# Column sums of a 32x32 softmax on VectorE in place of a masked fp32 product on TensorE

## The chip, the core and the metric

The kernel runs on one core of a Trainium2 chip. The core has four engines that matter here, each with its own instruction queue worked in order: TensorE (PE: matmuls, with its weight loads shown apart as PEld), VectorE (DVE), ScalarE (ACT) and GpSimd (POOL, which here only builds masks and issues DMAs). SyncE (SP) issues DMAs alone. TensorE writes to PSUM; the other compute engines bring the results to SBUF. The metric is the device time of one execution in microseconds (us).

## The reference, cut to what matters

Eight batches of eight heads go through a Nystrom attention with 32 landmarks, and its output through an MLP with a squared ReLU.

```python
A  = sm(q, k_lm)       # 576 x 32
Bm = sm(q_lm, k_lm)    # 32 x 32, softmax over its rows
C  = sm(q_lm, k)       # 32 x 576
Z  = Bm.transpose(0, 1, 3, 2) / (np.linalg.norm(Bm, ord=1, axis=(-2, -1), keepdims=True)
                                 * np.linalg.norm(Bm, ord=np.inf, axis=(-2, -1), keepdims=True) + 1e-06)
for _ in range(6):
    Z = 2 * Z - Z @ Bm @ Z
attn = A @ Z @ C @ v
out  = square(maximum(attn_rows @ w_in, 0)) @ w_out
```

The change concerns the starting scale of `Z`. Each row of `Bm` sums to one, so the `inf` norm is one up to rounding, and the kernel uses the 1-norm alone: the largest column sum of each 32x32 matrix.

## The kernel before, in words

**Layout.** The eight heads of a batch lie as two groups of four: partition 32a+i, group qd holds row i of head 4*qd+a. `BB` is an fp32 tile of 128 x 2 x 2 x 32: `BB[:, 1]` holds the landmark softmax (rows on partitions), `BB[:, 0]` its transpose in blocks of 32x32 (line 288). `blk` is the 128 x 128 block-diagonal mask of ones (four blocks of 32), in fp32, and `blk_bf` the same in bf16.

**Stages of a batch.** `attention(b)` is a generator. It makes the segment means (line 244), the landmark scores (line 274, `Exp` on ACT at line 277), the softmax (lines 283 to 288 on DVE), then `inverse_begin` and `inverse_first`, three `joint_step`s, one `last_joint_step` and two `newton_step`s, with the large scores (line 392), sums, transposes and the product with `v` (`c_values`, line 453) as side work between them. Its result is `G` (line 575 and its copies at 581 to 589), with which `mlp_in(b)` makes `h` on PE (line 603), `r` on ACT (line 609) and the square `gT` on DVE (line 610). `mlp_out(b)` multiplies `gT` by `w_out` (line 632, 16 matmuls of 128x512 to one output tile).

**Order.** Batch 0's attention runs alone at the start, in the order in which it is written (three engines are on a manual schedule there), with small filler matmuls (`warm`, line 201) in PE's gaps. From then on `mlp_in(b)` and `mlp_out(b)` on PE are interleaved with `attention(b+1)`, by a loop that advances the generator a step at a time; the framework's scheduler settles the final order of the instructions. Batches 1 and 2 transpose q and k on PE (lines 218 and 228, copied out at 501 to 512); batches 3 to 7 have it done by DMA, issued from SP (lines 189 and 195) after DVE's `nat` copies (line 187), which are pinned behind the first joint step of the batch before.

**Buffers.** All small products and transposes share the PSUM tag `n`, three buffers in rotation. `h` has two, `ops` one, `r` (SBUF) three.

**The lines the change touches.** `inverse_begin` (lines 324 to 338) multiplies the fp32 mask by the fp32 softmax (line 326): `colps[p, qd, m]` is then the sum of column m of p's head, the same in all 32 rows of that head. DVE copies the transposed softmax to bf16 (`btc`, line 330), spreads it to a block-diagonal stationary operand (`BT`, line 307; batch 0 takes `btc` as it is, in 32x32 pieces), takes the maximum over m from PSUM (`n1`, line 333), adds 1e-6 (line 335) and takes the reciprocal (`rc`, line 337). `inverse_first` multiplies `BT` by `btc` on PE (line 316, here called the nu product), scales the result and the softmax by `rc` (lines 343 and 345, `EY`), and spreads the first half to `ED`, the stationary operand of the first joint step.

Of the kernel before, what the change touches and what calls it, by code (L numbers as in the profile page):

```python
# [8 lines left out]
P = 128  # L9
AF = mybir.ActivationFunctionType  # L10
ALU = mybir.AluOpType
AX = mybir.AxisListType

BF16 = mybir.dt.bfloat16
F32 = mybir.dt.float32
# [5 lines left out]
M = 32  # L21
# [13 lines left out]
def kernel(  # L35
# [9 lines left out]
    nc = tc.nc  # L45

    const = ctx.enter_context(tc.tile_pool(name="const", bufs=1))
# [3 lines left out]
    small = ctx.enter_context(tc.tile_pool(name="small", bufs=2))  # L51
# [64 lines left out]
    def band(t, pattern, base, mult):  # L116
        return nc.gpsimd.affine_select(out=t, in_=t, pattern=pattern, compare_op=ALU.is_ge,
                                       fill=0.0, base=base, channel_multiplier=mult)
# [11 lines left out]
    mask4 = const.tile([P, 4], F32, name="mask4")  # L130
    nc.vector.memset(mask4[:], 1.0)
    band(mask4[:], [[-32, 4]], 0, 1)
    masked = band(mask4[:], [[32, 4]], 31, -1)
    blk = const.tile([P, 4, M], F32, name="blk")
    nc.vector.tensor_copy(blk[:], mask4[:, :].unsqueeze(2).to_broadcast([P, 4, M]))
    blk_bf = const.tile([P, 4, M], BF16, name="blk_bf")
    nc.vector.tensor_copy(blk_bf[:], blk[:])
    ones_bf = const.tile([P, 1], BF16, name="ones_bf")
    nc.vector.memset(ones_bf[:], 1.0)

# [31 lines left out]
    def ntile(shape, dt=F32):  # L172
        return psum.tile(shape, dt, tag="n", bufs=3, name="n")
# [30 lines left out]
    def attention(b: int, R: dict):  # L204
# [61 lines left out]
        BB = small.tile([P, 2, 2, M], F32, tag="BB", name="BB")  # L266
# [27 lines left out]
        def stationary(src, tag):  # L294

            if first:
                if src.dtype == BF16:
                    return src
                res = newt.tile([P, 2, M], BF16, tag="U", name="U")
                nc.vector.tensor_copy(res[:], src)  # L300
                return res[:]
            res = (small if tag == "BT" else newt).tile([P, 2, 4, M], BF16, tag=tag, name=tag)
            spread(res, src)
            return res.rearrange("p q a m -> p q (a m)")

        def spread(dst, src):
            nc.vector.tensor_tensor(dst[:], src.unsqueeze(2).to_broadcast([P, 2, 4, M]),  # L307
                                    blk_bf[:].unsqueeze(1).to_broadcast([P, 2, 4, M]), ALU.mult)

        def products(diagonal, moving):  # L310
            n, w = moving(0).shape[-1], diagonal.shape[-1]
            res = ntile([P, 2, n])
            with nullcontext():
                for qd in range(2):
                    for a in range(0, P, w):
                        nc.tensor.matmul(res[a:a + w, qd, :], lhsT=diagonal[a:a + w, qd, :],  # L316
                                         rhs=moving(qd)[a:a + w], start=True, stop=True)
            return res
# [3 lines left out]
                                                  op0=ALU.mult, op1=ALU.subtract)  # L322

        def inverse_begin():
            colps = ntile([P, 2, M])
            nc.tensor.matmul(colps.rearrange("p a m -> p (a m)"),
                             lhsT=blk.rearrange("p a m -> p (a m)"),
                             rhs=BB[:, 1, :, :].rearrange("p a m -> p (a m)"), start=True, stop=True)
            btc = small.tile([P, 2, M], BF16, tag="btc", name="btc")
            nc.vector.tensor_copy(btc[:], BB[:, 0, :, :])  # L330
            BT = stationary(btc[:], "BT")
            n1 = small.tile([P, 2], F32, tag="n1", name="n1")
            nc.vector.reduce_max(n1[:], colps[:], axis=AX.X)
            c1 = small.tile([P, 2], F32, tag="c1", name="c1")
            nc.vector.tensor_scalar(out=c1[:], in0=n1[:], scalar1=1e-6, scalar2=None, op0=ALU.add)
            rc = small.tile([P, 2], F32, tag="rc", name="rc")
            nc.vector.reciprocal(rc[:], c1[:])
            return btc, BT, rc

        def inverse_first(btc, BT, rc):  # L340
            rcb = rc[:, :].unsqueeze(2).to_broadcast([P, 2, M])
            nu = products(BT, lambda qd: btc[:, qd, :])
            nc.vector.tensor_tensor(EY[:, :, 0, :], nu[:], rcb, ALU.mult)
            ED = stationary(EY[:, :, 0, :], "ED")
            nc.vector.tensor_tensor(EY[:, :, 1, :], BB[:, 1, :, :], rcb, ALU.mult)
            return BT, ED

# [18 lines left out]

        def b_times_v(BT, v):
            nu = products(BT, lambda qd: v[:, qd, :])
            return stationary(nu[:], "ED")
# [93 lines left out]
        if first:  # L463
# [17 lines left out]
            act(*q1)  # L481
            scores("k", 0)
            BT, ED = inverse_first(*inverse_begin())
            scores("q", 0)
            side = [[(scores, "q", 1), (a_sums, 0, 0)],
# [7 lines left out]
        else:  # L493
# [6 lines left out]
            if b < DMA_T:  # L500
                dve(*transposed("q", 0))
            yield
            begun = inverse_begin()
            yield
            BT, ED = inverse_first(*begun)
# [48 lines left out]
        for qd in range(2):  # L554
            nc.tensor.matmul(wt[:, qd, :], lhsT=cvb.rearrange("p q d -> p (q d)"), rhs=zt[:, qd, :],
                             start=True, stop=True)
# [9 lines left out]
        for n in range(4):  # L566
            with tc.issue_after(mark[0].ins) if n == 2 and mark else nullcontext():
# [5 lines left out]
                for p in range(NPAIR):  # L573
                    for i in range(2):
                        nc.tensor.matmul(g[i][M * p:M * p + M, :],  # L575
                                         lhsT=WT[64 * i:64 * i + 64, i, M * p:M * p + M],
                                         rhs=w_in_bf[64 * i:64 * i + 64, p, n * 512:n * 512 + 512],
                                         start=True, stop=True)
# [162 lines left out]
```

The softmax here doesn't subtract the row's maximum and nothing guards it: scores larger than these inputs give would overflow.

## Time and profile before

| what | value |
|---|---|
| four executions | 272.94, 272.95, 273.63, 276.85 us; median 273.29 |
| the profiled execution | 273.25 us, of which 271.5 are the span from its first to its last instruction |
| DVE busy | 173.7 us of the span |
| ACT busy | 157.5 us |
| mean granted TensorE clock | 0.993 |
| line 330, `btc` copy on DVE | 8 times, 183 to 195 ns |
| line 345, `EY` from the softmax on DVE | 8 times, 215 to 226 ns |
| line 610, `gT` on DVE | 128 times, mean 454 ns |

Times in the tables and views are in us from the first instruction unless marked ns. In a timeline a row gives the start, the time from the start of the first to the end of the last of its merged instructions, the engine, the line, the operation, the tiles (out<-in), the shape and a count; in square brackets stands the engine's idle time before it and what ended that. Matmuls overlap in PE's pipeline, so the pace of a stream of them is read from their starts, not from their durations: four matmuls of line 603 take 0.65 us together at 0.286 each, so one starts every (0.65 - 0.286)/3 = 0.12 us; two of line 632 take 0.59 at 0.38 each, so one starts every 0.21 to 0.22 us. Batches are counted from 0.

### The profile page before, as it was taken

The page shows a single profiled execution, that of the slowest core. Times are in us where ns is not written, and L with a number is a line of the kernel's source. Part 1 is how long each engine was busy: PE and PEld are TensorE (multiplying, and loading weights), DVE is VectorE, ACT ScalarE, POOL GpSimd, SP SyncE. Part 2 cuts the span into 40 slices and gives each one's busy share as a digit, 9 for nine tenths or more (in the row PEclk, how much of TensorE's full clock was granted, in tenths as well). Part 3 has the DMA queues.
Part 4 walks back from the last instruction along what each step waited for, and adds up shares of the span by engine and source line. Part 5 has one row for each costly group of instructions (what it writes and reads, how often), then busy time and mean ns, then how long its engine had stood idle before and what let it go on. Part 6 is the DMA issues. An engine that isn't in the chain of part 4 may idle for free.

```text
span 271.5 us, 7312 instructions
## 1 busy us (share of the span) xinstructions
PE 257.2 (95%) x3067; PEld 153.1 (56%) x3067; DVE 173.7 (64%) x482; ACT 157.5 (58%) x274; POOL 42.5 (16%) x66
## 2 busy tenths in 40 slices
PE   2968999999999999999999999999999999999994
PEld 1845675466654655556654665466645665466444
DVE  3685888757794569646974669548964759545100
ACT  2553887366935677367926576467826674567211
POOL 3652433310420202201220120200000000000000
PEclk9997999999999999999999999999999999999999
DMA  7999999999799999999599929994831011111032
GB/s 200 221 201 198 202 206 190 211 206 155 93 143 127 181 113 140 172 107 176 113 181 111 193 60 153 174 150 80 170 64 57 24 41 41 77 41 40 18 100 77
DMA packets 69793, 35.34 MB, mean 130 GB/s; under 512 B 37376, under 2 KB 64256, under 8 KB 69760
## 3 DMA queue, kind: packets, MB, share of 16 engines
q0 software_dynamic: 37696, 17.17, 55.9%
q1 hardware_dynamic: 26816, 8.39, 24.0%
q10 hardware_dynamic: 5248, 9.31, 10.8%
q8 instruction: 24, 0.39, 0.6%
q14 instruction: 9, 0.07, 0.1%
HBM read 36.70 MB, written 9.44 MB: 170 GB/s over the span
## 4 chain that ended last, share of the span: by engine, by line
PE 74%; DVE 10%; DMA 10%; ACT 3%; issue 1%; DVEq 0%; ACTq 0%
PE ops L632 30%; PE h L603 18%; DMA T<-nat 8%; PE n L632 8%; PE g L575 3%; DVE gT L610 2%; PE n L316 2%; DMA raw<-in_k_dram 2%; PE n L453 2%; DVE ra L417 2%; PE n L244 2%; PE n L392 2%; PE n L434 2%; ACT r L609 2%; PE idle L201 2%
## 5 line engine op out<-in xcount | busy, mean ns | idle before, releaser
L632 PE MATMUL ops<-w_out_bf,gT 128*128 128x512 bf16 (+1 forms) x480 | 121.6, 372 | 0.1
L609 ACT ACTIVATE r<-h 128x576 bf16<-128x576 f32 x128 | 81.9, 652 | 33.8 <-PE h L603 27.4
L603 PE MATMUL h<-AT,G 128*128 128x288 bf16 x512 | 83.4, 286 | 0.7 <-ACT G L581 0.3
L610 DVE TENSOR_TENSOR gT<-r 128x576 bf16<-128x576 bf16 x128 | 57.8, 454 | 40.8 <-ACT r L609 39.5
L632 PEld LDWEIGHTS <-gT 128*128 128x128 bf16 x592 | 53.6, 98 | 40.4 <-issue 6.2
L603 PEld LDWEIGHTS <-G 128*128 128x128 bf16 x512 | 45.6, 98 | 20.2 <-issue 2.0
L641 ACT COPY o_sb<-ops 128x512 f32<-128x512 f32 (+1 forms) x29 | 16.7, 578 | 35.3 <-PE ops L632 35.2
L632 PE MATMUL n<-w_out_bf,gT 128*128 128x512 bf16 x112 | 29.6, 380 | 0.0
L589 DVE CAST G<-g 128x1024 bf16<-128x1024 f32 x14 | 17.1, 1225 | 13.2 <-PE g L575 13.2
L587 ACT CAST G<-g 128x1024 bf16<-128x1024 f32 x14 | 14.2, 1012 | 9.4 <-PE g L575 8.9
L438 ACT COPY AT<-n 128x576 bf16<-128x576 bf16 x9 | 5.8, 639 | 15.8 <-PE n L434 13.1
L392 PE MATMUL n<-bd,T 128*128 128x64 bf16 x256 | 13.5, 193 | 0.2
L392 PEld LDWEIGHTS <-T 128*128 128x128 bf16 x256 | 11.3, 98 | 4.1 <-DMA T<-nat 0.5
L316 PEld LDWEIGHTS <-ED 128*128 128x128 bf16 x84 | 6.7, 97 | 11.8 <-DVE ED L307 8.2
L424 DVE TENSOR_TENSOR an<-EA,rra 128x640 bf16<-128x640 f32 (+2 forms) x18 | 13.3, 739 | 0.0
L417 DVE TENSOR_REDUCE ra<-EA 128x20 f32<-128x640 f32 (+2 forms) x18 | 13.0, 720 | 0.0
L84 POOL DMA_DIRECT2D qkt<-in_k_dram x7 | 4.9, 693 | 47.2 <-PE n L254 30.1
L106 POOL DMA_DIRECT2D vm<-in_v_dram x8 | 7.0, 881 | 30.7 <-PE n L453 27.4
L96 POOL DMA_DIRECT2D raw<-in_k_dram x7 | 6.5, 928 | 30.8 <-DVE ED L307 19.0
L244 PEld LDWEIGHTS <-nat 128*128 128x128 bf16 x256 | 8.8, 97 | 3.3 <-DVE nat L187 0.2
L396 ACT ACTIVATE EA<-n 128x512 f32<-128x512 f32 x16 | 9.7, 605 | 1.4 <-PE n L392 1.4
L396 ACT ACTIVATE EC<-n 128x512 bf16<-128x512 f32 x16 | 9.6, 603 | 1.2 <-PE n L392 1.1
(116 smaller groups left out, 277.6 us busy)
## 6 DMA issues: line engine op xcount, KB each, us to landing
out_dram<-o_sb ACTq DMA_DIRECT2D x31, 256.0 KB, 4.1
vm<-in_v_dram POOLq DMA_DIRECT2D x8, 512.0 KB, 15.8
raw<-in_k_dram POOLq DMA_DIRECT2D x7, 512.0 KB, 10.5
raw<-in_q_dram POOLq DMA_DIRECT2D x7, 512.0 KB, 14.1
w_in_bf<-in_moe_w_in_dram POOLq DMA_DIRECT2D x4, 512.0 KB, 10.5
w_out_bf<-in_moe_w_out_dram POOLq DMA_DIRECT2D x4, 512.0 KB, 16.0
out_dram<-o_sb ACTq DMA_DIRECT2D x9, 128.0 KB, 2.4
raw<-in_k_dram SPq DMA_DIRECT2D x1, 1024.0 KB, 5.8
```

Source lines behind the costliest of these rows:

```text
L244: nc.tensor.matmul(means[:, ti, p, :], lhsT=src.rearrange("p h d -> p (h d)"), rhs=seg[:, c + (ti if c == NC4 else 0), :], start=(n == 0 a ...
L392: nc.tensor.matmul(sc[:, c, j, :, :], lhsT=X[nm + "T"][:, c, p, :], rhs=BD[:, 1 if nm == "q" else 0, p, 0:64], start=True, stop=True)
L396: nc.scalar.activation((EA if nm == "q" else EC)[:, qd, 0:NC4, :], sc.rearrange("p c j i m -> p c (j i m)"), AF.Exp, scale=SCALE)
L417: nc.vector.reduce_sum(ras[i][:, lo:hi, :], EA[:, i, lo:hi, :].rearrange("p c (h m) -> p c h m", m=M), axis=AX.X)
L424: nc.vector.tensor_tensor(an[:, i, lo:hi, :].rearrange("p c (h m) -> p c h m", m=M), EA[:, i, lo:hi, :].rearrange("p c (h m) -> p c h m", ...
L587: nc.scalar.copy(dst, gg[:])
L589: last = nc.vector.tensor_copy(dst, gg[:])
L603: last = nc.tensor.matmul(h[:, j, 0:HALF], lhsT=G[:, qd, f * P:(f + 1) * P], rhs=AT[:, qd, j * HALF:(j + 1) * HALF], start=(qd == 0), stop ...
L609: nc.scalar.activation(r.rearrange("p (j t) -> p j t", j=2), h[:, :, 0:HALF], AF.Relu)
L610: return nc.vector.tensor_tensor(gT[:, f, o:o + S], r[:], r[:], ALU.mult)
L632: mark[:] = [nc.tensor.matmul(ops, lhsT=gT[:, f, t * P:t * P + P], rhs=w_out_bf[:, f, i * n:i * n + n], start=(f == 0), stop=(f == NF - 1))]
L641: nc.scalar.copy(o_h, ops)
```

## The change

The fp32 product is gone. The column sums are made on DVE from the transposed softmax: a sum along the free axis of `BB[:, 0]` (128 x 2 x 32 to 128 x 2) gives each partition the sum of its own column; a 32x32 transpose, fed with that sum repeated 32 times, lays the 32 sums of a head along the free axis of each of its partitions; the maximum is then taken from this SBUF tile and no longer from PSUM. The fp32 mask `blk` goes too, and `blk_bf` is made from `mask4` directly.

```diff
-    blk = const.tile([P, 4, M], F32, name="blk")
-    nc.vector.tensor_copy(blk[:], mask4[:, :].unsqueeze(2).to_broadcast([P, 4, M]))
     blk_bf = const.tile([P, 4, M], BF16, name="blk_bf")
-    nc.vector.tensor_copy(blk_bf[:], blk[:])
+    nc.vector.tensor_copy(blk_bf[:], mask4[:, :].unsqueeze(2).to_broadcast([P, 4, M]))
...
         def inverse_begin():
-            colps = ntile([P, 2, M])
-            nc.tensor.matmul(colps.rearrange("p a m -> p (a m)"),
-                             lhsT=blk.rearrange("p a m -> p (a m)"),
-                             rhs=BB[:, 1, :, :].rearrange("p a m -> p (a m)"), start=True, stop=True)
             btc = small.tile([P, 2, M], BF16, tag="btc", name="btc")
             nc.vector.tensor_copy(btc[:], BB[:, 0, :, :])
             BT = stationary(btc[:], "BT")
+            cs = small.tile([P, 2], F32, tag="cs", name="cs")
+            nc.vector.reduce_sum(cs[:], BB[:, 0, :, :], axis=AX.X)
+            rows = small.tile([P, 2, M], F32, tag="rows", name="rows")
+            nc.vector.transpose(rows[:], cs[:, :].unsqueeze(2).to_broadcast([P, 2, M]))
             n1 = small.tile([P, 2], F32, tag="n1", name="n1")
-            nc.vector.reduce_max(n1[:], colps[:], axis=AX.X)
+            nc.vector.reduce_max(n1[:], rows[:], axis=AX.X)
```

What the scheduler makes of it, by a comparison of both programs: on PE the product is gone from all eight batches. In batches 4 and 6 the nu product stands two line-603 matmuls later than before, and two fewer follow behind it. In batch 1 line-603 matmuls, up to three at a time, move behind steps of the attention that they preceded, among them the nu product; and on ACT the first of the transposed copies (line 508) comes one `r` earlier. In batches 0, 2, 3, 5 and 7 PE's order is otherwise the same. On DVE the sum always stands directly behind `btc`. In batches 2, 4 and 6 it takes the place that the maximum had ahead of `BT`; in batches 3, 5 and 7 the maximum stood behind `BT`, so that there the sum comes newly in front of it. The transpose, the maximum, the addition and the reciprocal follow `BT`, with one or two `gT` between them; in batch 0 they follow the sum at once. SP and POOL have the same instructions in the same order.

## The prediction

> **What bounds the kernel now.** I read the page first, then the product's own line, then PE's stretch around it in one batch, then the chain of waits at the two places where PE does stand still.
>
> ```profile
> PE 257.2 (95%) x3067; PEld 153.1 (56%) x3067; DVE 173.7 (64%) x482; ACT 157.5 (58%) x274; POOL 42.5 (16%) x66
> ...
> PEclk9997999999999999999999999999999999999999
> ...
> q8 instruction: 24, 0.39, 0.6%
> ```
>
> PE is busy for 95% of the span and nearly all its idle time lies in the first 31 us; from there to the end a microsecond less of PE work is worth up to a microsecond. DVE has slack on average, which says nothing about the moments at which PE waits for it. The product itself, by its line:
>
> ```profile
> L326 PEld LDWEIGHTS n<-BB,blk x16: 186/190/190, 14.2 to 214.2; 128*128 128x128 f32 x16
> L326 PE MATMUL n<-BB,blk x16: 219/275/323, 14.3 to 214.3; 128*128 128x64 f32 x16
> ```
>
> Sixteen of each for eight batches: the fp32 product runs as two loads and two matmuls. Its durations overlap its neighbours, so what it costs is read from the starts. PE's timeline in batch 4:
>
> ```profile
> 124.43 0.41 PE L603 MATMUL h<-AT,G 128*128 128x288 bf16 x2
> 124.71 0.43 PE L326 MATMUL n<-BB,blk 128*128 128x64 f32 x2
> 124.98 0.41 PE L603 MATMUL h<-AT,G 128*128 128x288 bf16 x2
> 125.23 0.59 PE L632 MATMUL ops<-w_out_bf,gT 128*128 128x512 bf16 x2
> 125.66 0.29 PE L603 MATMUL h<-AT,G 128*128 128x288 bf16 x1
> 125.95 0.21 PE L316 MATMUL n<-btc,BT 128*128 128x32 bf16 x2
> ```
>
> Two line-603 matmuls from 124.43, at 0.12 each, would let the next one start at 124.67; it starts at 124.98. The product costs 0.31 us here. The nu product (L316) could start at 125.66 + 0.12 = 125.78 and starts at 125.95: PE waits 0.17 for DVE's `BT`.
>
> DVE's prices, grouped by line (mean of one after the busy time):
>
> ```profile
> L288 DVE STREAM_TRANSPOSE BB<-BB 128x64 f32<-128x64 f32 x8 | 2.0, 244 | 0.2
> L333 DVE TENSOR_REDUCE n<-n 128x2 f32<-128x64 f32 x8 | 1.8, 224 | 0.2
> ...
> L283 DVE TENSOR_REDUCE rs<-Eb 128x2 f32<-128x64 f32 x8 | 1.7, 215 | 0.9 <-ACT Eb L277 0.8
> ```
>
> **What the change takes away.** Batches 1, 4 and 6 have the product between line-603 matmuls: 0.31 us each as above (batch 1: 37.28 - 36.83 - 0.12 = 0.33). In batches 2, 3, 5 and 7 it stands behind a line-632 matmul; in batch 2 it starts at 61.70, when the next matmul could have started, and that one starts at 61.87: 0.17 each. Together 3 x 0.31 + 4 x 0.17 = 1.61 us of PE's pace, batch 0 apart.
>
> **What it adds on DVE.** A sum of the form of line 283 (0.215 us, from SBUF too) and a transpose of the form of line 288 (0.244), with the pauses between dependent instructions (from 60.46 to 60.71 for the sum, 61.17 to 61.45 for the transpose): 0.25 + 0.28 = 0.53 us a batch. The maximum goes from 0.224 to about 0.215 by reading SBUF. The input of the transpose is one value repeated; the scaling of line 286, which repeats an operand in the same way, takes 223 ns, so I give the repetition nothing; the bounds are 0 and, if the transpose were as slow as the 128x256 line 307 from the same engine, 0.04 more. The removed `blk` copy (0.22 us at 7.20) frees DVE before a wait of 0.50 for a DMA at 8.18: nothing.
>
> One rule of the Trainium skill speaks against the change: "VectorE: DVE Perf Modes", section on the rules for kernel authors, wants the number of chained DVE instructions kept small, since each pays a fixed cost; its errata table gives 58 cycles plus the elements at 0.96 GHz, an estimate of 0.13 us for 64 elements. Rows 283 and 288 show 0.215 and 0.244, so the rule holds and its figure is low; by it the addition would be 0.25 instead of 0.53 us, and the sum below would stay as it is.
>
> **Batch 0.** Here DVE is the path: the chain of waits goes through L333, L335, L337, L343, L345 to the first joint step at 15.86. Without the product, DVE goes straight from `btc` (ends 14.63) to the sum; the maximum starts at 14.65 + 0.53 = 15.18 instead of 14.71. The first joint step comes 0.46 us later. The cover is this:
>
> ```profile
> 19.15 0.31 PE n L453 x20
> 19.46 1.30 issue
> ```
>
> PE stands 1.30 us in `c_values` without any waiting semaphore in the profile. I read it as missing code: the instruction queue brought 24 packets of 0.39 MB together, 16 KB each, one for every 256 of PE's 6134 instructions; the trace's packet records have its first at 18.33 to 19.26, and PE goes on at 20.76. The stall lies 448 instructions into the program; the fetch's trigger, if it is 256 instructions earlier, lies at 13.4, before anything that the change moves. Then the 0.46 us vanish in the stall: PE arrives at 19.92 and still waits to 20.76. DVE's own backlog (`an` and `U` to 20.37, then idle until 21.45) has 1.08 us of room. Cost taken: 0; if the stall moves along instead, 0.46.
>
> **Batch 1** (DVE is packed from 36.3 to 40.6, PE idles 0.2 to 0.25 at several places on `r`, `h` and `n` buffers). Gain of at most 0.31; DVE's 0.53 can come back through `BT` and the transposed copies. `BT` itself gets one `gT` (0.35) out of its way and one sum (0.25) into it, and the nu product has three matmuls fewer ahead of it, so it waits for `BT`, and the three matmuls are done behind it. I take 0.2 of gain, bounds 0.31 and -0.5.
>
> **Batch 2.** `BT` ends at 63.31, the nu product starts at 63.37 after a wait of 0.45 (its place would be 62.92). The DVE instructions before `BT` are as many and as long as before. PE arrives 0.17 earlier and waits 0.17 longer: 0.
>
> **Batch 3.** The nu product has no wait (`BT` ends at 94.45, product at 95.61), so 0.17 are gained at 94.3 and lost at once:
>
> ```profile
> 75.17 21.38 DMA T<-nat
> 96.55 0.05 issue
> 96.59 0.41 PE n L392 x8
> ```
>
> The DMA transpose of q, issued at 75.17 behind batch 2's first joint step, lands when PE has already waited 0.23 us for it. It moves with batch 2, not with batch 3: 0 (bound: 0.17, if it lands earlier).
>
> **Batches 4 and 6.** 0.31 less, two matmuls (0.24) earlier done: PE reaches the nu product at 125.78 - 0.31 + 0.24 = 125.71 and waits for the same `BT` to 125.95, but has those two matmuls behind it: 0.24 each, bounds 0.17 and 0.31. **Batches 5 and 7** as batch 3, without a late DMA (the transposed q of batches 4 to 7 lands about 4 us or more before its use): 0.17 each. In all of them `rc` and the first `ED` come about 0.5 later; `ED` is ready at 96.8 and 127.05 for joint steps at 99.55 and 128.90, so 2.7 and 1.8 us of room cover it; without that room PE would wait 0.5 a batch.
>
> Sum: 0 + 0.2 + 0 + 0 + 2 x 0.24 + 2 x 0.17 = 1.0 us. The profiled execution's 273.25 (span 271.5 and 1.75 around it), 0.04 from the median, becomes **272.2**.
>
> **Rivals.** *DVE takes it back* (273.2): batch 1 loses 0.5, the stall of batch 0 moves along by 0.46; 0.82 - 0.96 is about 0. For it: DVE is packed there. Against: the room counted above. Chance 0.2.
>
> *The clock* (271.4). Windows of the granted clock:
>
> ```profile
> 18.50:21.90 3.40, 1.95 (x105) 1.00 1.12 210
> 21.90:25.40 3.50, 3.50 (x38) 0.51 1.37 194
> ```
>
> After a stretch with 1.95 us of PE in 3.40 the clock is at half for the next, with the filler matmuls and transposes of batch 0's end on the path. If 0.46 us less of stall in the first stretch keep the clock up, about half of the path's PE work there is saved, 1.6 us by its pieces from 21.77 to 25.27, less what DVE's chain then sets; between 0 and 1.6 I take 0.8: 271.4. The other way, 0.46 us more idle time at 15.4 could halve the stretch from 18.5, at a similar price up. The skill's "TensorE: Matmul & The Clock Gate", on its two states, asks for a whole idle window of 3.4 us before the clock falls; the row shows it falling after a stretch of which 57% was busy, so the row decides; by the page the stall would not matter and this rival would fall away. Chance 0.13.
>
> *Slower: the transposed q of batch 3* (275.9). PE waits for this one DMA already, it is the longest of ten (4.3 to 21.4 us to landing, median 10.2), and it competes with loads that DVE and PE release in the batches whose order changes. If one more 0.52 MB load gets ahead of it at the 150 GB/s of that stretch (slices at 75 to 95 us: 143, 127, 181), it lands 3.5 us later: 273.25 + 3.5 - 0.82 = 275.9. It decides from 0.8 us of lateness on. For it: no slack there. Against: the DMA queues' orders are unchanged. Chance 0.17; the forecast keeps 0.5, with 271.7 to 272.7 of its own.
>
> **Numbers.** Most of the late DMA's chance above 274.8 and a little at the low end are left out: 271.0 to 274.8. I call 1% (2.7 us) what a measurement here can tell. Faster than 270.56 needs the clock's full price and every bound of the sum: 0.08. Slower than 276.0 is half of the late DMA and some unforeseen reordering: 0.12.
>
> **What would show it.** Line 326's rows gone, and on DVE 8 sums near 0.22 and 8 transposes near 0.24; the stall in `c_values` shorter by about 0.4, ending near 20.8; the wait for `T` in batch 3 longer than 0.23; from 97 us on PE's marks drifting ahead by 0.8 until the end. Wrong if the stall keeps its 1.3 us, if PE waits for `ED` in a first joint step, or if `T` lands at another distance from its issue.

## The result, and the profile after

The changed kernel takes 272.79 us (median of 46 runs) against 273.55 for the kernel before (70 runs). The ratio is 0.9974, 95% interval 0.9965 to 0.9984, so the gain is 0.71 us, between 0.44 and 0.96: clear of the noise, and well inside the 1% that the prediction took as the least that can be told. The forecast of 272.2 lies 0.6 below; 0.3 of that is the base, whose median over 70 runs is 273.55 while the prediction started from the profiled 273.25, and the rest is a gain of 0.7 instead of 1.0.

The profiled execution has a span of 270.6 us, 0.9 less than before. The page of the changed kernel, the lines that answer to those shown before (engine busy, granted clock, instruction queue):

```profile
PE 254.3 (94%) x3051; PEld 150.3 (56%) x3051; DVE 174.7 (65%) x497; ACT 157.7 (58%) x274; POOL 42.6 (16%) x66
...
PEclk9999999999999999999999999999999999999999
...
q8 instruction: 24, 0.39, 0.6%
```

PE has 16 matmuls and 16 loads fewer, DVE 15 instructions more (8 sums, 8 transposes, less the mask's copy). The slice of half clock near 24 us is gone in this execution. The new DVE instructions and their neighbours, grouped by line (busy time, mean ns of one):

```profile
L329 DVE STREAM_TRANSPOSE rows<-cs 128x64 f32<-128x64 f32 x8 | 1.9, 239 | 0.0
L331 DVE TENSOR_REDUCE n<-rows 128x2 f32<-128x64 f32 x8 | 1.7, 215 | 0.2
L327 DVE TENSOR_REDUCE cs<-BB 128x2 f32<-128x64 f32 x8 | 1.7, 213 | 0.0
```

These are the forecast prices (0.215, 0.244, and 0.215 for the maximum from SBUF), and the repeated operand costs the transpose nothing. The rule page drawn on before, "VectorE: DVE Perf Modes" of the Trainium skill, corrects its own table in its section on the TRN2 errata: it measures a fixed term of about 150 cycles in place of 58. An estimate from that is (150 + 64)/0.96 GHz = 0.223 us, which the measured 0.213 to 0.239 bears out.

### The profile page after: what moved, and what is told of

Its sections match the earlier page's. It is cut to its first block, busy times and chain, and to the rows that moved or that the text cites. A ratio compares the mean times of both kernels' runs of the same rounds, so it can differ in the third digit from the quotient of the medians.

```text
span 270.6 us, 7294 instructions
## 1 busy us (share of the span) xinstructions
PE 254.3 (94%) x3051; PEld 150.3 (56%) x3051; DVE 174.7 (65%) x497; ACT 157.7 (58%) x274; POOL 42.6 (16%) x66
## 4 chain that ended last, share of the span: by engine, by line
PE 69%; DVE 15%; DMA 10%; ACT 3%; issue 1%; SPq 0%; POOL 0%; DVEq 0%
PE ops L630 31%; PE h L601 16%; PE n L630 9%; DMA raw<-in_q_dram 5%; DVE gT L608 4%; DMA vm<-in_v_dram 3%; PE g L573 3%; DVE ra L415 2%; DMA qkt<-in_q_dram 2%; PE n L314 2%; ACT r L607 2%; PE n L451 2%; PE n L242 2%; PE n L390 1%; DVE an L422 1%; PE n L432 1%
## 5 line engine op out<-in xcount | busy, mean ns | idle before, releaser
L390 PEld LDWEIGHTS <-T 128*128 128x128 bf16 x256 | 11.3, 98 | 3.7
L185 DVE COPY nat<-raw 128x2048 bf16<-128x2048 bf16 x14 | 9.5, 688 | 1.5 <-DMA raw<-in_q_dram 0.9
```

The lines of the kernel that those rows point to most:

```text
L390: nc.tensor.matmul(sc[:, c, j, :, :], lhsT=X[nm + "T"][:, c, p, :], rhs=BD[:, 1 if nm == "q" else 0, p, 0:64], start=True, stop=True)
```

## Where PE gains and loses, from start to end

The start of a given matmul is a mark that can be compared between kernels. The table gives each kernel's marks minus those of the kernel before, in us (negative: earlier), one profiled execution each; the kernels are described in the section after this one. "h0" is the first line-603 matmul, "S1", "S2" and "S4" the landmark scores of batches 1, 2 and 4 (line 274), "L3" the large scores of batch 3 (line 392), which need the DMA-transposed q, "end" the last matmul. The kernel before has them at 26.90, 34.54, 59.32, 96.59, 122.97 and 267.83. At S2, L3, S4 and the end PE has done the same matmuls in all kernels, the fp32 product apart. At S1 it has not: in the change it has done one line-603 matmul fewer than before (0.12 us), in sums_twice and b0_slow five fewer (0.60 us), because the scheduler moved them to later.

| kernel | h0 | S1 | S2 | L3 | S4 | end | S4 to end |
|---|---|---|---|---|---|---|---|
| before_again | -1.53 | 0.16 | 0.16 | 0.05 | 0.10 | 0.09 | -0.01 |
| after | -2.13 | 0.17 | 0.17 | -0.24 | -0.06 | -0.90 | **-0.84** |
| after_again | -0.09 | 0.29 | 0.57 | 0.16 | 0.34 | -0.51 | **-0.85** |
| after_third | -0.10 | 0.51 | 0.50 | 1.13 | 1.13 | 0.31 | **-0.82** |
| late_only | -2.64 | -0.09 | -0.10 | 0.58 | 0.58 | -0.20 | **-0.78** |
| early_only | 0.16 | 0.56 | 0.99 | 2.58 | 2.58 | 2.70 | 0.12 |
| dead_product | -1.55 | -0.02 | 0.01 | -0.11 | 0.07 | -0.17 | -0.24 |
| sums_twice | -0.85 | 0.08 | 0.55 | 0.15 | 0.33 | -0.49 | **-0.82** |
| b0_slow | 0.42 | 0.34 | 1.60 | 1.20 | 1.38 | 0.55 | **-0.83** |
| copy_later | -0.66 | 1.03 | 1.46 | 0.43 | 0.62 | -0.21 | **-0.83** |
| b0_keeps | -0.30 | -0.30 | 0.12 | -0.28 | -0.09 | -0.92 | **-0.83** |
| copy_later_2 | 0.17 | 0.64 | 0.63 | 1.10 | 1.11 | 0.28 | **-0.83** |
| b0_keeps_copy_2 | 0.21 | 0.21 | 0.64 | 0.31 | 0.31 | -0.51 | **-0.82** |

The last column is the sum 2 x 0.24 + 2 x 0.17 = 0.82 of the prediction: every kernel whose batches 4 to 7 are those of the change has it within 0.04. All the scatter, from 0.3 us early to 2.6 late, arises before S4, most of it by S2 and at L3.

PE's and DVE's timelines of the changed kernel in batch 4 (start, time, engine, line, operation) show how the 0.25 us of such a batch come about; they differ from the prediction in one place:

```profile
124.37 0.65 PE L601 MATMUL h<-AT,G 128*128 128x288 bf16 x4
124.86 0.59 PE L630 MATMUL ops<-w_out_bf,gT 128*128 128x512 bf16 x2
125.29 0.41 PE L601 MATMUL h<-AT,G 128*128 128x288 bf16 x2
125.77 0.21 PE L314 MATMUL n<-btc,BT 128*128 128x32 bf16 x2
125.83 0.41 PE L601 MATMUL h<-AT,G 128*128 128x288 bf16 x2
```

```profile
125.20 0.19 DVE L324 CAST btc<-BB 128x64 bf16<-128x64 f32 x1
125.30 0.21 DVE L327 TENSOR_REDUCE cs<-BB 128x2 f32<-128x64 f32 x1
125.43 0.28 DVE L305 TENSOR_TENSOR BT<-btc,blk_bf 128x256 bf16<-128x256 bf16 x1
125.63 0.24 DVE L329 STREAM_TRANSPOSE rows<-cs 128x64 f32<-128x64 f32 x1
```

The four matmuls at 124.37 now run through, without the product's hole. PE could start the nu product (line 314 here) at 125.29 + 2 x 0.12 = 125.53 and starts it at 125.77, so it waits 0.24 for `BT`, as forecast. But only **one** line-603 matmul has moved in front of it: two follow it here, three before. The description of the order and the prediction, which both said two, counted one too many. The other half of the gain is `BT` itself. DVE in the kernel before, in batch 4 and, for comparison, in batch 2, and the three matmuls in batch 4:

```profile
125.25 0.19 DVE L330 CAST btc<-BB 128x64 bf16<-128x64 f32 x1
125.47 0.23 DVE L333 TENSOR_REDUCE n<-n 128x2 f32<-128x64 f32 x1
125.62 0.28 DVE L307 TENSOR_TENSOR BT<-btc,blk_bf 128x256 bf16<-128x256 bf16 x1
126.02 0.53 PE L603 MATMUL h<-AT,G 128*128 128x288 bf16 x3
```

```profile
62.42 0.19 DVE L330 CAST btc<-BB 128x64 bf16<-128x64 f32 x1
62.52 0.22 DVE L333 TENSOR_REDUCE n<-n 128x2 f32<-128x64 f32 x1
```

`BT` starts 0.23 after `btc` in the change; before, with the maximum between them, 0.37. The product was done by 125.14 (124.71 + 0.43), yet the maximum started only at 125.47, after the end of `btc` (125.44), while the sum starts 0.10 after the start of `btc` and overlaps it. Why the maximum did not overlap is not known: in batch 2 the same instruction, which reads PSUM and follows PE there too, starts 0.10 after `btc`, so neither the source nor PE's semaphore prevents it everywhere. So 0.12 (one matmul) + 0.13 (`BT` earlier) = 0.25; the prediction's 2 x 0.12 gave the same number by another road.

## The experiments

Ratios are to the kernel before on the same chip, with 95% intervals.

**Repeats.** The two kernels unchanged, one execution each (before_again, after_again), and the change timed once more on another chip (after_third).

> The kernel before, profiled once more. Question: do the 1.30 us stall of PE in batch 0's product with v and the half clock behind it belong to this kernel, or to one execution? Theory (the stall is code that comes late, its moment set by the DMA traffic at the start): a stall at the same matmul, of 0 to 2 us, and the start of line 274 in batch 1 within 0.4 us of 34.54 whether or not it is there, since the loads of batch 1 set it. Rival (the stall is fixed in the old order of PE and sets what follows): 1.2 to 1.4 us again, half clock again, and batch 1 later by the same amount as the first h matmul.

> The changed kernel, profiled once more. Theory: with or without a stall in batch 0, line 274's matmul of batch 1 starts within 0.4 us of 34.71, and from there to the end the marks stand against the kernel before as in the first profile: level to batch 3, then 0.25, 0.17, 0.25 and 0.17 us earlier in batches 4 to 7, together 0.84. Rival (the gain comes from the start, where this profile showed neither stall nor half clock): if the stall comes back, the end is later by 1 us or more.

> The changed kernel, timed on the same chip as the next three, so that they are compared with it and not with the record of other chips. All theories: 0.7 us faster than before, 0.3 to 1.1. Its profile shows whether batches 4 to 7 give 0.84 us a fourth time.

The single executions took 273.32 us for the kernel before and 272.73 for the change; both have S1 within the forecast 0.4, and the change has its 0.85 from S4 to the end. after_third was 0.9986 (0.9953 to 1.0018), which contains the first result and, alone, also no change. The repeats also show the start. The stall of 1.30 us in `c_values`, on which the prediction rested batch 0, is in none of the three profiles of the change, but neither is it in before_again. It came back in two kernels below that keep the product in batch 0. PE's timeline of b0_keeps there, its idle time and what ended it in brackets:

```profile
19.38 0.20 PE L460 MATMUL n<-vm,EC 128*32 128x64 bf16 x4
...
20.55 0.21 PE L460 MATMUL n<-vt,ect 128*32 128x64 bf16 x4 [0.97 <-issue]
```

It stands at the same instruction, the first with `vt` (as in before, and at 21.03 after 0.96 us in b0_keeps_copy_2). The traces' packet records bear out the reading as late code. The first packet of the instruction queue ends at 19.26 us in before, 19.14 in b0_keeps and 19.58 in b0_keeps_copy_2, later than in any other profile (17.0 to 18.7), and PE goes on 1.51, 1.41 and 1.45 us after it; in the other eleven PE comes to this instruction 1.46 us or more after the packet, and does not stall. So the stall depends on when the packet lands and when PE arrives, and it came in three of fourteen executions. All three have the product and the old chain in batch 0; nine profiles have the longer chain there and no stall.

The clock at the start varies in the same way. Windows of after_again (length, then PE's, PEld's, DVE's, ACT's and POOL's busy time, the granted clock, DMA share, GB/s):

```profile
12.30:15.70 3.40, 1.89 (x43) 1.53 (x41) 2.82 (x12) 2.35 (x5) 2.77 (x4) 1.00 1.30 193
15.70:19.10 3.40, 2.95 (x47) 1.86 (x48) 2.08 (x8) 1.48 (x4) 1.63 (x2) 0.51 1.35 205
19.10:22.60 3.50, 3.50 (x117) 2.01 (x114) 3.04 (x12) 0.60 (x1) 0.74 (x1) 0.50 1.12 212
```

Here the clock is halved for two windows; in the change's first profile and in before_again it is whole from 11.3 and 11.9 us on, in before it was halved for one. The skill's "TensorE: Matmul & The Clock Gate", in Part 1, has the gate's window run freely, so that the phase differs from run to run; these rows agree with that, but the fall again follows a window in which PE was busy for 1.89 of 3.40 us, not an idle one as the page's table of states asks.

**Which batches carry the gain.** Sums on DVE in batches 4 to 7 only (late_only), and in 0 to 3 only (early_only); the others keep the product. Core of the edit (early_only has `b < 4`):

```diff
+            new = b >= 4
+            if not new:
+                colps = ntile([P, 2, M])
+                nc.tensor.matmul(colps.rearrange("p a m -> p (a m)"),
...
+            if new:
+                cs = small.tile([P, 2], F32, tag="cs", name="cs")
...
-            nc.vector.reduce_max(n1[:], rows[:], axis=AX.X)
+            nc.vector.reduce_max(n1[:], rows[:] if new else colps[:], axis=AX.X)
```

> Column sums on DVE in batches 4 to 7, the fp32 product kept in batches 0 to 3. Theory (the gain is PE's pace in batches 4 to 7): 0.8 us faster than before, 0.6 to 1.0, as fast as the full change. Rival 1 (the gain comes from the start of the run): no difference, within 0.3. Rival 2 (it is spread over all batches by the count of products): half of the full change, 0.35 to 0.5 us.

> Column sums on DVE in batches 0 to 3, the fp32 product kept in batches 4 to 7. Theory: what PE gains in batches 0 to 3 goes into waits for loads (batch 1), for BT (batch 2) and for the transposed q (batch 3): within 0.3 us of before. Rival 1 (the start): 0.7 us faster, like the full change. Rival 2 (spread): 0.35 to 0.5 us faster. Rival 3 (the reordered batch 1 costs): 0.3 to 0.5 us slower.

late_only: 0.9955 (0.9929 to 0.998), 1.2 us faster (0.5 to 1.9). early_only: 1.0017 (0.9986 to 1.0047), 0.5 us slower (-0.4 to +1.3). The late half carries the gain; the early half shows none, and may cost something: 1.2 less 0.5 is the 0.7 of the whole change. late_only is not shown to beat the change, since the intervals overlap. Part of what early_only shows in its profile is not its own: the chain of waits (start, length, what) has the transposed q of batch 3 late.

```profile
76.12 23.01 DMA T<-nat
99.13 0.05 issue
99.17 0.41 PE n L399 x8
```

The transfer took 23.0 us from its issue, and PE waited 1.8 us for it. This is the mechanism of the "slower" rival. But late_only, whose batches 0 to 3 are those of the kernel before, has the same transfer at 22.03 us with 0.8 us of PE waiting; after_third waits 0.9, while after, after_again and dead_product do not wait. The lateness occurs in both kernels; these profiles do not show it as a cost of the change. On time, it is worth little: in after the large scores start 0.24 earlier than before, but 0.18 of this is lost by batch 3's next joint step, because line 630's matmuls must wait for ACT's copy out of the one `ops` buffer, which ends at 97.47 (96.89 + 0.58) in both profiles.

**The product or the sums.** dead_product is the kernel before with the sums added and used; the product is computed and its result not read. sums_twice is the change with a second pair of sum and transpose, whose result is the one used.

dead_product, against the kernel before (the matmul of line 326 stays):

```diff
             BT = stationary(btc[:], "BT")
+            cs = small.tile([P, 2], F32, tag="cs", name="cs")
+            nc.vector.reduce_sum(cs[:], BB[:, 0, :, :], axis=AX.X)
+            rows = small.tile([P, 2, M], F32, tag="rows", name="rows")
+            nc.vector.transpose(rows[:], cs[:, :].unsqueeze(2).to_broadcast([P, 2, M]))
             n1 = small.tile([P, 2], F32, tag="n1", name="n1")
-            nc.vector.reduce_max(n1[:], colps[:], axis=AX.X)
+            nc.vector.reduce_max(n1[:], rows[:], axis=AX.X)
```

sums_twice, against the change:

```diff
+            cs2 = small.tile([P, 2], F32, tag="cs2", name="cs2")
+            nc.vector.reduce_sum(cs2[:], BB[:, 0, :, :], axis=AX.X)
+            rows = small.tile([P, 2, M], F32, tag="rows2", name="rows2")
+            nc.vector.transpose(rows[:], cs2[:, :].unsqueeze(2).to_broadcast([P, 2, M]))
```

> The changed kernel, with the fp32 product put back in all batches and its result not used. It prices the product on PE alone. Theory: 0.8 us slower than the changed kernel (0.17 to 0.31 us in each of batches 4 to 7, nothing in 0 to 3), so level with the kernel before, within 0.3. Rival (what helped was that n1 no longer waits for PE, not PE's time): as fast as the changed kernel, 0.7 faster than before.

> The changed kernel, with the sum and the transpose done twice in every batch (the first result not used): DVE has 0.46 us of instructions more per batch, 0.53 with pauses. It prices DVE's share. Theory (DVE's room covers it: loads in batch 0, 1.8 to 2.7 us of room before the first joint step in batches 3 to 7): within 0.4 us of the changed kernel; in batches 2, 3, 5 and 7 and wherever the second sum and transpose stand ahead of BT, PE waits for BT up to 0.5 longer in batches 2, 4 and 6. Rival (DVE is level with PE in each batch): 0.5 us a batch, 3 to 4 us slower.

dead_product: 1.001 (0.9981 to 1.0038), level with the kernel before, as the theory had it, and the interval excludes the 0.7 us of the rival. Its timeline in batch 4:

```profile
124.50 0.41 PE L607 MATMUL h<-AT,G 128*128 128x288 bf16 x2
124.78 0.43 PE L326 MATMUL n<-BB,blk 128*128 128x64 f32 x2
125.06 0.41 PE L607 MATMUL h<-AT,G 128*128 128x288 bf16 x2
...
125.90 0.21 PE L316 MATMUL n<-btc,BT 128*128 128x32 bf16 x2
```

```profile
125.33 0.19 DVE L330 CAST btc<-BB 128x64 bf16<-128x64 f32 x1
125.43 0.21 DVE L333 TENSOR_REDUCE cs<-BB 128x2 f32<-128x64 f32 x1
125.56 0.28 DVE L307 TENSOR_TENSOR BT<-btc,blk_bf 128x256 bf16<-128x256 bf16 x1
```

The product's hole is back at its price (124.50 + 0.24 = 124.74 to 125.06: 0.32), and `BT` is early (0.23 after `btc`). So this kernel has half of batch 4's gain and half of batch 6's: 2 x 0.12 = 0.24, the very number in the table's last column. This separates the two halves named above.

sums_twice: 1.0012 (0.998 to 1.0044). The theory had it near the change, and the timed ratio does not confirm that: it lies 0.4% above the change's, with an interval that just reaches it. From S4 on, though, it has the full -0.82, so in batches 4 to 7 another 0.5 us of DVE work per batch costs nothing. If the second pair costs time, it does so in batches 0 to 3; the profile is 0.4 behind the change there, no more than the repeats differ.

**Does a delay of batch 0 pass?** b0_slow adds four transposes to batch 0's chain, each undoing or redoing the one before (about 1.1 us). b0_keeps has the change everywhere but in batch 0, whose product stays. b0_slow's edit against the change:

```diff
+            if first:
+                for t in range(4):
+                    turned = small.tile([P, 2, M], F32, tag="turned%d" % t, name="turned")
+                    nc.vector.transpose(turned[:], rows[:])
+                    rows = turned
```

For b0_keeps the edit is that of late_only with this line:

```diff
+            new = b >= 1
```

> The changed kernel, with four more dependent 32x32 transposes in batch 0 between the transpose of the sums and the maximum (an even number gives the same values back): 4 x 0.28 = 1.1 us more on the path of the first inverse. Theory (batch 1's load of q bounds the start; PE waited for it for 0.75 us after a start 2.1 us ahead): within 0.3 us of the changed kernel, the first h matmul later by 0.3 to 1.1 and the wait for batch 1's copies shorter by as much. Rival (batch 0's chain bounds the start): 1.0 us slower.

> Column sums on DVE in batches 1 to 7, the fp32 product kept in batch 0, whose path to the first inverse is then 0.46 us shorter than in the changed kernel. Theory (batch 0 is ahead of batch 1's loads in some executions and behind them in others, so its 0.46 us are paid in part): 0 to 0.4 us faster than the changed kernel. Rival 1 (always covered): no difference, within 0.1 in the mark of batch 1's landmark scores. Rival 2 (never covered): 0.4 to 0.5 us faster.

b0_slow: 1.0022 (0.999 to 1.0053), 1.3 us above the change's 0.9974 (with b0_slow's own interval, 0.4 to 2.2), where the theory had at most 0.3 and the rival 1.0. It fits the rival, but it is not the price of the delay alone, because the scheduler also orders batch 1 differently in this kernel, on PE and DVE. From S1 to S2 it falls back by 1.26 us: 0.60 are the five matmuls that it still had to do at S1, and 0.60 a wait of PE that the change does not have, for a reciprocal of the product with `v` that here stands behind other work on DVE:

```profile
48.52 0.83 DVE L427 TENSOR_TENSOR an<-EA,rra 128x640 bf16<-128x640 f32 x1
...
49.42 0.13 DVE L461 RECIPROCAL rc<-n 128x2 f32<-128x2 f32 x1
49.55 0.21 PE L314 MATMUL n<-v,BT 128*128 128x32 bf16 x2 [0.60 <-DVE rc L461]
```

b0_keeps: 0.9972 (0.9937 to 1.0007) on the chip on which the change had 0.9986: 0.4 us better with intervals of 0.9 us each, so no difference is shown. Its profile is the earliest of all at S1 (-0.30), but it too has another order in batch 1, with a wait of 0.54 for the same reciprocal, and S2 comes at 0.12. Neither kernel isolates batch 0. The marks say this much: at S1 the six profiles whose batches 0 and 1 are those of the change (the three of the change, early_only, copy_later, copy_later_2) lie at 0.17 to 1.03, mean 0.53; the five with the old chain in batch 0 lie at -0.30 to 0.21, mean 0.00.

What stands between batch 0 and S1 is seen in the change's own timeline. It reaches h0 2.1 us ahead of the kernel before, and at S1 nothing is left:

```profile
29.21 0.69 DVE L185 COPY nat<-raw 128x2048 bf16<-128x2048 bf16 x1 [0.55 <-DMA raw<-in_k_dram]
...
31.92 0.69 DVE L185 COPY nat<-raw 128x2048 bf16<-128x2048 bf16 x1 [0.91 <-DMA raw<-in_q_dram]
32.67 0.56 PE L242 MATMUL n<-seg,nat 128*128 128x32 bf16 x16 [0.75 <-DVE nat L185]
```

The segment means of batch 1 wait for DVE's copy, and the copy for the load of q. Over the fourteen profiles h0 lies anywhere from 24.25 to 27.32 us; these second segment means start between 32.48 and 33.53 (without copy_later, by 33.19). Where PE is early, it waits for the load; in before, with h0 at 26.90, it had no wait there. So the cover of batch 0 is batch 1's load, and it is used up in a slow start; the means above suggest that on average most of the added time passes.

**A copy in DVE's way in batch 2.** In the change PE waits 0.61 us for `BT` in batch 2 (by the starts, 63.53 - 62.80 - 0.12; the 0.45 in brackets counts from the end of the matmul before), where a transposed copy (line 499) and a `gT` stand in front of `btc`:

```profile
61.62 0.69 DVE L499 COPY T<-n 128x1024 bf16<-128x1024 bf16 x1
62.23 0.45 DVE L608 TENSOR_TENSOR gT<-r 128x576 bf16<-128x576 bf16 x1
62.59 0.19 DVE L324 CAST btc<-BB 128x64 bf16<-128x64 f32 x1
...
63.53 0.21 PE L314 MATMUL n<-btc,BT 128*128 128x32 bf16 x2 [0.45 <-DVE BT L305]
```

copy_later puts the first half of q's transposes and copies behind `inverse_begin` in batches 1 and 2; copy_later_2 does so in batch 2 alone; b0_keeps_copy_2 adds batch 0's product to that. The edit of copy_later:

```diff
             yield
+            begun = inverse_begin()
+            yield
             if b < DMA_T:
                 dve(*transposed("q", 0))
             yield
-            begun = inverse_begin()
-            yield
             BT, ED = inverse_first(*begun)
```

> The changed kernel, with the transposes of q's first half and their copy to SBUF (0.69 us on DVE) behind inverse_begin instead of in front of it in batches 1 and 2. PE's wait of 0.61 us for BT in batch 2 has this copy ahead of it on DVE. Theory: the wait goes, 0.3 to 0.6 us faster than the changed kernel in batch 2's marks, and since the transposed q of batch 3 is issued behind batch 2's first joint step, it comes earlier by as much, so that 0.3 to 0.5 us reach the end: 1.0 to 1.3 us faster than before. Rival (the transfer's landing is set by the DMA traffic): the gain is lost at line 392 in batch 3, level with the changed kernel.

> The changed kernel, with the transposes of q's first half and their copy behind inverse_begin in batch 2 alone. When it was moved in both batches, batch 2's nu product came 0.74 us earlier against the marks before it, and batch 1 lost 0.45. Theory: 0.6 to 0.75 us gained between the landmark scores and the nu product of batch 2, kept to batch 3's line 392 but for what the transposed q of batch 3 takes (0.4 there when both were moved): 0.3 to 0.7 us faster than the changed kernel. Rival (the DMA takes it all): level.

> Both of the last two edits. If both theories hold, 0.3 to 1.1 us faster than the changed kernel and 1.0 to 1.8 faster than before; if the start is always covered and the DMA takes batch 2's gain, level with the changed kernel.

The scheduler leaves batch 1 as it was in both copy_later and copy_later_2: the traces have the same instructions in the same order on every engine, so the two are one program, measured twice. copy_later: 0.9969 (0.9945 to 0.9994); copy_later_2: 0.9973 (0.9949 to 0.9997); b0_keeps_copy_2: 0.9962 (0.993 to 0.9993). Batch 2 of copy_later_2:

```profile
62.08 0.20 DVE L324 CAST btc<-BB 128x64 bf16<-128x64 f32 x1
...
62.32 0.28 DVE L305 TENSOR_TENSOR BT<-btc,blk_bf 128x256 bf16<-128x256 bf16 x1
...
62.83 0.59 PE L634 MATMUL ops<-w_out_bf,gT 128*128 128x512 bf16 x2
63.26 0.20 PE L314 MATMUL n<-btc,BT 128*128 128x32 bf16 x2
```

`BT` is done 0.66 us before PE comes to it, and from the landmark scores of batch 2 to its nu product the kernel gains 0.74 us. It keeps none of it at batch 3: its large scores start 1.10 us later than in before, after 1.3 us of waiting for the transposed q. copy_later did not wait there, but fell back by 0.43 from S1 to S2. That was not the move, which did not change batch 1, but one execution: `btc` and the sum take 0.63 and 0.52 us instead of 0.20 and 0.21, and both end when POOL's issue of a load ends, at 39.12.

```profile
38.24 0.88 POOL L96 DMA_DIRECT2D raw<-in_q_dram  x1 [1.61 <-DVE BB L284]
38.49 0.63 DVE L324 CAST btc<-BB 128x64 bf16<-128x64 f32 x1
38.60 0.52 DVE L327 TENSOR_REDUCE cs<-BB 128x2 f32<-128x64 f32 x1
```

The same is seen in early_only (0.63 and 0.53) and after_again (0.48 and 0.38), and in no other profile; there `btc` started 0.24 to 0.39 us after POOL's issue did. All three kernels of this group are faster than the kernel before; their intervals overlap each other and the change's, so none is shown to beat it, and the forecasts of a gain over the change are not confirmed.

## Why the prediction was right, and where its sum was off

**Batches 4 to 7, 0.82 us: right in size,** ten profiles with 0.78 to 0.85. In 5 and 7 the mechanism is as put (0.17 each). In 4 and 6 the term was right and its working was not: one matmul instead of two moved, and "the same `BT`" came 0.13 earlier, because the sum ahead of it overlaps `btc`, as the maximum did not there. The two errors cancelled; that the number 0.24 came out is luck.

**Batch 1, +0.2: mis-sized.** From S1 to S2 after, after_third and copy_later_2 gain 0.00 to 0.01 by the marks, 0.12 with the one matmul that they still had to do at S1. after_again, early_only and copy_later lose 0.28, 0.43 and 0.43, with the lengthened `btc` and sum shown above. The bound of -0.5 was not reached. What takes the product's 0.31 us back is seen in after:

```profile
39.52 0.23 DVE L341 TENSOR_TENSOR EY<-n,rc 128x64 bf16<-128x64 f32 x1
39.80 0.61 PE L216 MATMUL n<-ident_bf,nat 128*128 128x128 bf16 x8
40.45 1.01 ACT L510 COPY T<-n 128x1024 bf16<-128x1024 bf16 x1
41.51 0.22 PE L314 MATMUL n<-EY,ED 128*128 128x64 bf16 x2
```

`EY` needs the later `rc` and must read the nu product before that one of the three `n` buffers is free for the last eight transposes; they start 0.05 us after it, ACT copies them, and the first joint step follows that copy by 0.05, in all eight profiles with this order. Before, these transposes started 0.34 after `EY` and did not wait. `EY` ends 5.04 us after S1 in after and 4.73 before: 0.31 later. So DVE's added work comes back through a PSUM buffer and the transposed copies; the prediction had named the copies as one way.

**Batch 0, 0: the cover was wrongly named, and it is partial.** The added time is right but 0.1 too large: from the start of `btc` to that of the maximum are 0.28 us in before and 0.64 in after, 0.36 more and not 0.46, since the sum starts 0.11 after the start of `btc`, before its recorded end. The cover was to be the code stall. It is code, as the prediction read it, but it is missing in most profiles, with the product and without it, and the mark "ending near 20.8" can therefore be neither right nor wrong. The cover that is there is the load of batch 1, and the mean of S1 (0.53 later) suggests that most of the added time passes, so that this term, put at 0, was too small. 0.82 + 0.17 (batch 3) - 0.3 would be the measured 0.7; that the 0.3 come from batches 0 and 1 is an argument: S2 at 0.17 to 1.46 in the six profiles of the change's code, against -0.10 to 0.16 in three of the old, allows it and more, and how it parts between the two batches stays open.

**Batches 2 and 3.** In batch 2 PE waits 0.61 for `BT` instead of 0.45; that is the 0.17 that it comes earlier: 0, as put. In batch 3 the nu product gained its 0.17 in after; T's wait, which was to take it back, did not occur there, so the mark "longer than 0.23" failed in that execution, and held in after_third (0.9). The sign "if `T` lands at another distance from its issue" did come true (20.7 in after, 21.4 before), but before_again has 21.1: the distance varies in both kernels.

**The rivals.** DVE took back batch 1's gain but not the rest. The clock rival came true in the change's profile, whose clock is whole at the start, and its price was wrong: 2.1 us at h0 end in the wait for batch 1's load. Of the change's 46 runs, the 18 with a mean clock of at least 0.9985 have a median of 272.59, the 24 between 0.985 and 0.9985 one of 272.94: some 0.35 us, not 0.8. (The other four, lower still, took 273.97 to 275.34.) The slower rival's transfer does come late by up to 1.8 us, without regard to the change. In batches 1 to 7 PE never waited for `ED` in a first joint step, so the room of 1.8 to 2.7 us in batches 3 to 7 covered the later `rc` there; twice the added work left 0.43 of it in batches 4 and 6.

## What to carry to other kernels

On a PE-bound stretch, price a small matmul by the hole it leaves in the starts of its neighbours, and look at what its consumer stands in front of on the other engine: here half of the gain in two batches was that the instruction ahead of `BT` now overlapped the one before it. An edit to one batch can make the scheduler order another one differently, or do nothing at all: compare the orders before reading a difference. Before a stall is used as cover, see it in a second execution. A gain at the start of a kernel counts only up to the next load that does not move with it.

## What the runs showed of the hardware

PE's stall in `c_values` (1.30, 0.97 and 0.96 us) comes at one fixed instruction in some executions and is absent in others. The skill's "Runtime: NRT & Kernel Launch", section on instruction fetch, holds sequential fetching to be hidden by the issue rate; in these three executions it was not, since PE went on 1.41 to 1.51 us after the first instruction packet had landed, and in the other eleven PE came 1.46 us or more after it. The granted clock at the start of one and the same kernel was whole, halved for one window or halved for two, and the DMA transpose of batch 3's q ended a wait of PE in 7 of 14 profiles, 21.1 to 23.0 us after its issue. In 3 of 11 executions with the sums in batch 1, `btc` (0.48 to 0.63 us instead of 0.20) and the sum (0.38 to 0.53 instead of 0.21) ended together with POOL's DMA issue; a cause was not tested.
